# First feed-forward layer by seven block products in place of eight, summed in PSUM

## The chip, the cores and the metric

The kernel runs on one core of a Trainium2 chip. The metric is the device time of one execution in microseconds (us), the median of three runs. Engines are named as the profile names them: PE (TensorE matmuls), PEld (its weight loads), DVE (VectorE), ACT (ScalarE), POOL (GpSimd), SP (SyncE, which issues DMAs). L123 is line 123 of the kernel.

## The reference

A linear attention gives `x` (2304 tokens of 512), a layer of eight experts picks one expert per token, and a feed-forward pair with a gelu in the middle gives the output:

```python
x = _moe_ref(x=attention(q, k, v, omega), w_gate, w1, w2)   # one of 8 experts per token, 512 -> 1024 -> 512
h = x @ w_in                                                # 2304 x 512 by 512 x 2048
g = h * (1.0 / (1.0 + np.exp(-1.702 * h)))
return (g @ w_out).astype(np.float32)                       # 2304 x 2048 by 2048 x 512
```

`w_in` and `w_out` come as 64-bit floats.

## The kernel before

The program has three stages: attention, the experts, and the two feed-forward layers. Each product of float32 quality is three matmuls: an operand is split into a rounded high half (ACT copies it as type fp32r) and the low half that is left (DVE subtracts, `split`, L825 and L826), and high × high, high × low and low × high are summed in PSUM (`mm3`, L123).

The experts (`moe_gen`) go through four batches of 576 tokens in halves of 288. At the end of a half `y` is multiplied by the gate (DVE, L756), ACT rounds it to `yh` (L759), POOL, in the last batch DVE, makes `yl` (L761), and SP stores both in `y_dram` (L766).

The first layer (`first`) takes one of 16 feature tiles of 128 (`wi`) and one of five chunks of tokens (512, 512, 512, 480, 288 columns) and runs 4 × 3 matmuls into one bank of sums, `f_ps`. ACT applies the gelu into `g` (L1016) and stores `g` in `g_dram` (L1017) from its own DMA queue. 80 such pieces make 960 matmuls. Seven banks of PSUM take turns as `f_ps`, and four buffers as `g`. The first few pieces are allowed to run while the experts are still at work, and the scheduler puts them there.

The second layer (`second`, L1070) already uses seven products for eight on 2 × 2 blocks: operands `gs` are sums and differences of blocks of `g` (tile `gt`, loaded by SP from `g_dram`), split by ACT and DVE, and the weights `wo` are seven mixes of the blocks of `w_out`.

Two sorts of jobs prepare this beside the matmuls. `prep_in` loads two tiles of `w_in` (`raw`), decodes the 64-bit floats on DVE (L804, L808, L811, into `dec`) and splits them into `wi`. `prep_out` loads two tiles of `w_out`, decodes them into `z`, mixes the blocks on POOL and stores seven results in `wo_dram`. `prep_w` reads these back and splits them. `load_y` loads a chunk of `y`. A `Runner` moves such jobs on: the program calls it between pieces of the layer, and a job says after how many calls it wants to go on (`yield 6`). All this sets the program order; a scheduler then orders each engine's instructions by priorities and dependences, `behind` keeps an instruction after the last n of its engine, and buffers with the same tag wait for one another (a tile whose tag is in use waits until its last reader is done).

## Time and profile before

| | |
|---|---|
| median of 3 runs | 788.44 us (787.87 to 788.46) |
| profiled execution | 786.61 us, of which the span of the trace is 784.8 us |
| granted clock of the PE, mean over the span | 0.991 of full speed |
| busy share of the span | PE 97%, PEld 91%, DVE 58%, ACT 39%, POOL 23% |
| start of the last expert matmul, last first-layer matmul | 402, 597 us |

The profiled execution is one of its own, so its durations are set against its own time. A granted clock of 1.00 in a stretch is the 2.4 GHz level. Busy shares are means over the three stages. The matmuls' shown durations overlap (the PE is pipelined), so the price of a row of equal matmuls is read from the spacing of their starts.

### The profile page before, as it was taken

What the parts mean: (1) busy time and instruction counts of PE and PEld (TensorE: products, weight loads), DVE (VectorE), ACT (ScalarE), POOL (GpSimd) and SP (SyncE); (2) the same over time, 40 slices, a digit from 0 to 9 for tenths busy, and PEclk for the clock granted to TensorE, in tenths of its full rate; (3) what the DMA queues carried; (4) which work ended last, traced back from release to release, by engine and by line L of the source; (5) the groups of instructions that cost most, each with busy time, mean ns of one, the idle gap of its engine ahead of it and who ended that gap; (6) DMA issues with size and microseconds to landing.
All of it is one profiled execution on the core that took longest, in us unless ns stands there. A gap on an engine that the chain in (4) does not pass through costs nothing.

```text
span 784.8 us, 14258 instructions
## 1 busy us (share of the span) xinstructions
PE 761.8 (97%) x5538; PEld 711.5 (91%) x5538; DVE 453.6 (58%) x1026; ACT 306.4 (39%) x575; POOL 178.8 (23%) x134
## 2 busy tenths in 40 slices
PE   7998899999999999999999999999999999999996
PEld 6877799999999999999998888888889999999996
DVE  5867876586775262644623756530135877777761
ACT  5545563454423342442212322532344433333340
POOL 3564296539402450110002433000000000000000
PEclk9999899999999999999999999999999999999998
DMA  5447676258723430458879999942575444444411
GB/s 160 120 120 179 183 214 161 81 152 234 138 73 104 144 105 31 147 160 291 288 261 346 329 381 342 357 157 101 173 222 175 135 134 136 135 134 134 134 28 30
DMA packets 150185, 136.00 MB, mean 173 GB/s; under 512 B 60768, under 2 KB 131680, under 8 KB 149216
## 3 DMA queue, kind: packets, MB, share of 16 engines
q1 hardware_dynamic: 138592, 116.16, 49.2%
q10 hardware_dynamic: 11520, 18.88, 6.6%
q8 instruction: 45, 0.74, 0.4%
q14 instruction: 28, 0.23, 0.1%
HBM read 83.41 MB, written 45.11 MB: 164 GB/s over the span
## 4 chain that ended last, share of the span: by engine, by line
PE 80%; DMA 7%; DVE 5%; issue 4%; POOL 1%; ACT 1%; SPq 1%; POOLq 0%; DVEq 0%; ACTq 0%
PE f_ps L123 24%; PE m_ps L123 18%; PE qa L1070 12%; PE qm L1070 6%; PE w_ps L123 3%; PE pb L1070 3%; PE kv_ps L385 3%; PE num L427 2%; DMA st<-in_moe_w_dram 2%; DMA gt<-g_dram 1%; PE pr L327 1%; DMA m<-in_q_dram 1%; PE tq L413 1%; DMA m<-in_k_dram 1%; PE pr L333 1%
## 5 line engine op out<-in xcount | busy, mean ns | idle before, releaser
L123 PE MATMUL f_ps<-y,wi 128*128 128x512 f32 (+2 forms) x960 | 199.2, 369 | 0.0
L123 PEld LDWEIGHTS f_ps<-y,wi 128*128 128x128 f32 x960 | 169.8, 188 | 28.3
L1070 PE MATMUL qa<-wo,gs 128*128 128x256 f32 x864 | 107.3, 282 | 0.0
L1070 PEld LDWEIGHTS qa<-wo,gs 128*128 128x128 f32 x864 | 104.9, 190 | 0.1
L1016 ACT ACTIVATE g<-f_ps 128x512 f32<-128x512 f32 (+2 forms) x80 | 44.0, 552 | 102.8 <-PE f_ps L123 83.6
L123 PE MATMUL m_ps<-xh,wh 128*128 128x288 f32 x256 | 78.9, 308 | 2.7 <-DVE h1l L706 1.7
L123 PE MATMUL m_ps<-xh,wl 128*128 128x288 f32 x256 | 76.8, 300 | 0.0
L123 PE MATMUL m_ps<-xl,wh 128*128 128x288 f32 x256 | 76.5, 299 | 0.0
L658 POOL TENSOR_TENSOR wl<-st,wh 128x1024 fp32r<-128x1024 f32 x23 | 54.5, 2376 | 44.7 <-ACT wh L656 44.7
L825 ACT ACTIVATE gs<-s 128x1024 fp32r<-128x1024 f32 x27 | 28.6, 1060 | 75.9 <-DVE s L1055 63.1
L342 DVE TENSOR_REDUCE small<-pr 128x4 f32<-128x512 f32 (+1 forms) x80 | 51.1, 639 | 10.8 <-PE pr L334 6.5
L706 DVE SCALAR_TENSOR_TENSOR h1l<-m_ps,h1h 128x288 fp32r<-128x288 f32 x64 | 28.8, 454 | 48.4 <-ACT h1h L703 48.2
L1070 PE MATMUL qm<-wo,gs 128*128 128x256 f32 x432 | 54.5, 283 | 0.4 <-DVE u L1086 0.4
L1070 PEld LDWEIGHTS qm<-wo,gs 128*128 128x128 f32 x432 | 52.8, 190 | 0.6 <-DVE u L1086 0.6
L123 PEld LDWEIGHTS m_ps<-xh,wh 128*128 128x128 f32 x256 | 48.7, 190 | 3.9 <-DVE h1l L706 2.3
L656 ACT ACTIVATE wh<-st 128x1024 fp32r<-128x1024 f32 (+1 forms) x33 | 34.0, 1031 | 41.7 <-DMA st<-in_moe_w_dram 23.3
L123 PEld LDWEIGHTS m_ps<-xl,wh 128*128 128x128 f32 x256 | 48.8, 190 | 0.2
L123 PEld LDWEIGHTS m_ps<-xh,wl 128*128 128x128 f32 x256 | 48.7, 190 | 0.0
L123 PE MATMUL m_ps<-h1h,wh 128*128 128x288 f32 x160 | 48.6, 305 | 0.0
L826 DVE TENSOR_TENSOR gs<-gt,gs 128x1024 fp32r<-128x1024 f32 x36 | 44.0, 1222 | 7.5 <-ACT gs L825 7.0
L123 PE MATMUL m_ps<-h1h,wl 128*128 128x288 f32 x160 | 47.8, 300 | 0.0
L123 PE MATMUL m_ps<-h1l,wh 128*128 128x288 f32 x160 | 47.7, 299 | 0.0
(156 smaller groups left out, 1422.7 us busy)
## 6 DMA issues: line engine op xcount, KB each, us to landing
gt<-g_dram SPq DMA_DIRECT2D x16, 1024.0 KB, 7.4
st<-in_moe_w_dram SPq DMA_DIRECT2D x31, 512.0 KB, 4.3
g_dram<-g ACTq DMA_DIRECT2D x48, 256.0 KB, 5.1
raw<-in_moe_w_in_dram SPq DMA_DIRECT2D x16, 512.0 KB, 5.8
raw<-in_moe_w_out_dram SPq DMA_DIRECT2D x16, 512.0 KB, 6.1
wo<-wo_dram SPq DMA_DIRECT2D x7, 1024.0 KB, 8.3
y<-y_dram SPq DMA_DIRECT2D x6, 1024.0 KB, 10.7
wo_dram<-z SPq DMA_DIRECT2D x8, 768.0 KB, 5.5
```

Of the source, the lines that this page charges most:

```text
L123: ins = nc.tensor.matmul(out=ps, lhsT=a, rhs=b, start=start and n == 0, stop=stop and n == 2)
L327: nc.tensor.matmul(out=ps[:, :, h2], lhsT=xT[:, (2 * pr + h2) * 2 + t0 // 2], rhs=wbd)
L342: nc.vector.tensor_reduce(out=pm, in_=ps[:, :w], axis=AX.X, op=ALU.max, negate=on_act)
L385: nc.tensor.matmul(out=kv_ps[:, h, :], lhsT=kp[j // 2][:, j % 2, h2, :], rhs=vm[:, h, t, :], start=(t == 0), stop=False,)
L427: nc.tensor.matmul(out=ps[:n, c, h2, :], lhsT=lhsT, rhs=kv[:, h, :])
L656: nc.scalar.activation(out=hi[:, :, s], in_=st[:, :, s], func=ACTF.Copy)
L658: eng.tensor_tensor(out=lo[:, :, s], in0=st[:, :, s], in1=f32(hi)[:, :, s], op=ALU.subtract)
L706: nc.vector.scalar_tensor_tensor(out=hl[:, f], in0=ps, scalar=0.0, in1=f32(hh[:, f]), op0=ALU.max, op1=ALU.subtract)
L825: nc.scalar.activation(out=hi, in_=src, func=ACTF.Copy)
L826: nc.vector.tensor_tensor(out=lo, in0=src, in1=f32(hi), op=ALU.subtract)
L1016: nc.scalar.activation(out=g, in_=ps, func=ACTF.Gelu_apprx_sigmoid)
L1070: ins = nc.tensor.matmul(out=ps, lhsT=x[:, f], rhs=w[i][:, f], start=start and f + m == 0, stop=f == NP - 1 and m == 2, skip_group_check=True,
```

## The change

Now the first layer too takes seven products for eight. The 2 × 2 blocks are: two feature tiles (j and j + 8, 128 features each), two halves of the 512 inputs, and two halves of 384 of a set of 768 tokens. A group (j, t) of the new `first` computes both feature tiles for set t: seven products (`PAIRS`) of 2 × 3 matmuls of 384 columns, 24 groups in all, 1008 matmuls. The sums of products are made in PSUM: product 1 in bank `qa` is copied by ACT into a second bank (`qn` or `qu`), products 6, 5 and 3 go on summing in `qa`, product 7 is copied out as `qs`, and DVE adds `qs` to `qa` once into bank `qt` (where product 4 goes on) and once into a tile `g`. The gelus go to two `g` tiles of 768 columns, `glo` and `ghi`, of a ring of three buffers, each stored whole. Two groups run interleaved. Three marking matmuls ahead of them let the sums go on in banks that an engine has written.

The weights are mixed and split by `prep_ins` (seven blocks per group of tiles, mixes on DVE for j of 0 and 1, else on POOL). `y` is now stored once in float32, without `yh` and `yl`; `prep_y` loads a set, mixes it into seven blocks on DVE and splits each, set 0 while the experts are at work, set 1 in memory that becomes free when they end. `prep_outs` replaces `prep_out` with a fixed pace, and the operands of the second layer take over the memory of sets and weights as they become free (`after_group`), two of the weight sets and three operand buffers only behind the last group. In the diff, lines of plain renaming are left out.

```diff
+    NH = 3 * P
+    NSET = NT // (2 * NH)
+    OUT_PACE = 6
...
-                def rest(y=y, yh=yh, yl=yl, dt=dt, hf=hf):
-                    nc.scalar.activation(out=yh, in_=y, func=ACTF.Copy)
-                    eng = nc.vector if b == B - 1 else nc.gpsimd
-                    eng.tensor_tensor(out=yl, in0=y, in1=f32(yh), op=ALU.subtract)
-                def store(yh=yh, yl=yl, dt=dt, hf=hf):
-                    for x, n, ch, o in pieces(b * S + hf * HS, HS):
-                        for i, t in enumerate((yh, yl)):
-                            nc.sync.dma_start(
-                                out=y_dram[ch][i][dt * P:(dt + 1) * P, o:o + n], in_=f32(t[:, x:x + n])
-                            )
-                lag(LAG_M, rest)
-                lag(3, store)
+                def store(y=y, dt=dt, hf=hf):
+                    x = 0
+                    while x < HS:
+                        ch, o = divmod(b * S + hf * HS + x, NH)
+                        n = min(HS - x, NH - o)
+                        nc.sync.dma_start(out=y_dram[ch][dt * P:(dt + 1) * P, o:o + n], in_=y[:, x:x + n])
+                        x += n
+                lag(2, store)
...
+    PAIRS = {
+        1: (W11, Y11), 2: (W12, Y21), 3: (WS4, Y22), 4: (W22, YT4), 5: (WS1, YT1), 6: (WS2, YT2), 7: (WS3, YT3),
+    }
...
+    def prep_ins():
+        for j in range(NP):
+            after = 4 if j < 2 else 0
+            raws = [load_raw(slots["ly"], 0, f, after) for f in (j, j + NP)]
+            yield IN_PACE
+            dec = slots["dec"].tile([P, 4, HALF], F32, tag="dec", name="dec", bufs=1)
+            mix = raws[0].bitcast(F32).rearrange("p (o c) -> p o c", c=HALF)
+            for n in range(2):
+                decode(dec[:, 2 * n:2 * n + 2].rearrange("p o c -> p (o c)").bitcast(I32), raws[n], HOLD)
+                yield 1
+            s1, s2, s4 = (mix[:, i] for i in range(3))
+            eng = nc.gpsimd if j > 1 else nc.vector
+            tt(eng, s1, dec[:, WS3], dec[:, W22], ALU.add)
+            tt(eng, dec[:, WS3], dec[:, W11], dec[:, WS3], ALU.subtract)
+            tt(eng, s2, s1, dec[:, W11], ALU.subtract)
+            tt(eng, s4, dec[:, W12], s2, ALU.subtract)
+            yield 3 if j > 1 else 1
+            while j % 3 >= len(slots["wi"]) or (j > 2 and through[j - 3] < NSET):
+                yield 1
+            pool, tag = slots["wi"][j % 3]
+            t = pool.tile([P, 14 * HALF], F32R, tag=tag, name="wi", bufs=1)
+            w = t.rearrange("p (s o c) -> p s o c", s=2, o=7)
+            for o, x in ((slice(0, 2), dec[:, 0:2]), (slice(2, 4), dec[:, 2:4]), (slice(4, 7), mix[:, 0:3])):
+                split(w[:, 0, o], w[:, 1, o], x)
+                yield 1
+            wi_t[j] = (w[:, 0], w[:, 1])
...
+    def prep_outs():
+        raws = slots["raw_o"]
+        def load(j):
+            for n, f in enumerate((j, j + NP)):
+                nc.sync.dma_start(out=raws[n], in_=w_out[f * P:(f + 1) * P, :])
+        load(0)
+        for j in range(NP):
+            yield OUT_PACE
+            z = slots["z"][:, j % 2]
+            zi = z.bitcast(I32)
+            for n in range(2):
+                decode(zi[:, 2 * n:2 * n + 2].rearrange("p a c -> p (a c)"), raws[n], HOLD)
+                yield 1
+            if j + 1 < NP:
+                load(j + 1)
+            for o, a, b, op in O_MIX:
+                tt(nc.gpsimd, z[:, o], z[:, a], z[:, b], op)
+            yield 2
+            nc.sync.dma_start(out=wo_dram[0, :, j], in_=z[:, 0])
+            nc.sync.dma_start(out=wo_dram[1:7, :, j].rearrange("o p d -> p o d"), in_=z[:, 2:8])
+            outs[0] += 1
...
+        x = slots["ly"].tile([P, 7, 2, NH], F32, tag="yt", name="yt", bufs=1)
+        for o, k, c in ((Y11, 0, 0), (YT3, 0, 1), (Y22, 1, 1), (Y21, 1, 0)):
+            ins = nc.sync.dma_start(
+                out=x[:, o], in_=y_dram[2 * t + c][k * DM // 2:(k + 1) * DM // 2].rearrange("(k p) n -> p k n", p=P)
+            )
+            behind(ins, after)
+        yield (6, 6, 13)[t]
+        eng = nc.vector
+        behind(tt(eng, x[:, YT1], x[:, YT3], x[:, Y11], ALU.subtract), HOLD)
+        tt(eng, x[:, YT3], x[:, Y22], x[:, YT3], ALU.subtract)
+        yield 1
+        tt(eng, x[:, YT2], x[:, Y22], x[:, YT1], ALU.subtract)
+        tt(eng, x[:, YT4], x[:, Y21], x[:, YT2], ALU.subtract)
+        while not home:
             yield 1
...
+        y = home[0]
+        for o in (YT3, YT2, Y11, Y21, YT1, YT4, Y22):
             yield 1
+            split(y[:, 0, o], y[:, 1, o], x[:, o], HOLD)
+        y_t[t] = (y[:, 0], y[:, 1])
...
+        home1.append(set_tile(hp, 1))
+        slots["wi"].append((hp, "wi2"))
+        jobs.queue.append(prep_y(2, [set_tile(hp, 2)]))
...
+        def marked(tag):
+            ps = bank_of(tag, 1, NH)
+            nc.tensor.matmul(out=ps, lhsT=y_t[0][0][:, 0, 0, 0:P], rhs=y_t[0][0][:, 0, 0])
...
+            def gelu(o, x):
+                nc.scalar.activation(out=o, in_=x, func=ACTF.Gelu_apprx_sigmoid)
+            c0, c1 = slice(0, NH), slice(NH, 2 * NH)
+            pa = bank_of("a", 3, NH)
+            product(1, pa, True)
+            pb = bank_of(("n", "u")[turns[0] % 2], 1, NH)
+            turns[0] += 1
+            nc.scalar.activation(out=pb, in_=pa, func=ACTF.Copy)
+            yield
+            pq = bank_of("m", 2, NH)
+            product(7, pq, True)
+            qs = hp.tile([P, NH], F32, tag="qs", name="qs", bufs=2)
+            nc.scalar.activation(out=qs, in_=pq, func=ACTF.Copy)
+            yield
+            product(6, pa, False)
+            pf = bank_of("t", 1, NH)
+            tt(nc.vector, pf, pa, qs, ALU.add)
+            yield
+            product(2, pb, False)
+            glo = hp.tile([P, 2 * NH], F32, tag="ob", name="g", bufs=3)
+            gelu(glo[:, c0], pb)
+            yield
+            product(5, pa, False)
+            ghi = hp.tile([P, 2 * NH], F32, tag="ob", name="g", bufs=3)
+            tt(nc.vector, ghi[:, c1], pa, qs, ALU.add)
+            yield
+            product(4, pf, False)
+            gelu(ghi[:, c0], pf)
+            gelu(ghi[:, c1], ghi[:, c1])
+            nc.scalar.dma_start(out=g_dram[t][1][j], in_=ghi)
+            yield
+            product(3, pa, False)
+            gelu(glo[:, c1], pa)
+            nc.scalar.dma_start(out=g_dram[t][0][j], in_=glo)
+            through[j] += 1
...
+        order = [(0, 0), (1, 0), (0, 1), (1, 1), (2, 0), (2, 1), (0, 2), (1, 2), (2, 2)]
+        order += [(j, t) for j in (3, 4) for t in range(NSET)]
+        order += [(j, t) for t in range(NSET) for j in (5, 6, 7)]
...
+            g = first(j, t)
+            for mine in (1, 0, 1, 0, 0, 1, 1):
+                if mine:
+                    next(g)
+                elif live is not None:
+                    next(live[0], None)
+                jobs()
+            if live is not None:
+                after_group(*live[1])
+            live = (g, (j, t))
+        for _ in range(3):
+            next(live[0], None)
             jobs()
+        wp.release()
+        wq = tc.alloc_tile_pool(name="wq", bufs=1)
+        gs_homes += [wq.tile([P, GSW], F32R, name=f"gs{i}") for i in range(2)]
+        g_homes.append(wq.tile([P, 2, NP, 2 * P], F32, name="gt1"))
+        p = hp.tile([P, SETW], F32R, tag="y2", name="p2", bufs=1)
+        jobs.queue += [prep_w(5, p[:, 0:WO], 3, 0), prep_w(6, p[:, WO:2 * WO], 4, 0)]
+        gs_homes.append(p[:, 2 * WO:2 * WO + GSW])
+        gts = {1: load_g(1)}
```

What this does to the order on the engines is shown at three places. **PE inside the first layer**, before: one feature tile (`f_ps`) with four chunks of tokens, named by their `y` tile, and the first matmul of the next.

```order
L123 MATMUL f_ps<-y_4658,wi 128x512 [waits Activation_49]
L123 MATMUL f_ps<-y_4658,wi 128x512 x11
L123 MATMUL f_ps<-y_4788,wi 128x512 [waits Activation_49]
L123 MATMUL f_ps<-y_4788,wi 128x512 x11
L123 MATMUL f_ps<-y_5071,wi 128x480 [waits Activation_49]
L123 MATMUL f_ps<-y_5071,wi 128x480 x11
L123 MATMUL f_ps<-y_5266,wi 128x288 [waits Activation_49]
L123 MATMUL f_ps<-y_5266,wi 128x288 x11
L123 MATMUL f_ps<-y_4656,wi 128x512 [waits Activation_49]
```

And after, six products of two interleaved groups, one on set 2 (`y_5142`), the next on set 0 (`y_3929`); `qa`, `qm`, `qt` and `qn` are banks. In turn these are product 5 of the first group, 7 of the second, 4 and 3 of the first, 6 and 2 of the second.

```order
L1068 MATMUL qa<-y_5142,wi 128x384 [waits DVE_49]
L1068 MATMUL qa<-y_5142,wi 128x384 x5
L1068 MATMUL qm<-y_3929,wi 128x384 x6
L1068 MATMUL qt<-y_5142,wi 128x384 [waits Activation_49]
L1068 MATMUL qt<-y_5142,wi 128x384 x5
L1068 MATMUL qa<-y_5142,wi 128x384 [waits DVE_49]
L1068 MATMUL qa<-y_5142,wi 128x384 x5
L1068 MATMUL qa<-y_3929,wi 128x384 [waits Activation_49]
L1068 MATMUL qa<-y_3929,wi 128x384 x5
L1068 MATMUL qn<-y_3929,wi 128x384 x6
```

Before, a piece waited only at its start, for the gelu that emptied its bank; after, products 5 and 3 wait for the DVE add that reads their bank, 6 for ACT's copy out of it, and 4 for an ACT instruction too.

**ACT at the end of the experts**, before: the last halves of `h1`, the last `yh`, then the first gelus of pieces whose matmuls are partly done.

```order
L703 ACTIVATE h1h<-m_ps 128x288 [waits PE_49] x4
L759 ACTIVATE yh<-y 128x288 [waits DMAHW0_49,DVE_49,Activation_49]
L759 ACTIVATE yh<-y 128x288 [waits DMAHW2_49,DVE_49,Activation_49]
L759 ACTIVATE yh<-y 128x288 [waits DMAHW0_49,DVE_49,Activation_49]
L759 ACTIVATE yh<-y 128x288 [waits DMAHW2_49,DVE_49,Activation_49]
L1016 ACTIVATE g<-f_ps 128x512 [waits DMAHW4_49,DMAHW5_49,DMAHW3_49,DMAHW6_49,DMAHW1_49,DMAHW7_49,DVE_49,PE_49]
L1016 ACTIVATE g<-f_ps 128x512
L1017 DMA g_dram<-g 128x512 [waits Activation_49] x2
```

And after (`y_5141` is set 1, `yt` its mixed blocks, `wi` from `dec` or `raw` the third tile of weights).

```order
L694 ACTIVATE h1h<-m_ps 128x288 [waits PE_49] x4
L1083 ACTIVATE qn<-qa 128x384 [waits PE_49]
L810 ACTIVATE wi<-dec 128x512 [waits DMAHW3_49,DMAHW4_49,DMAHW2_49,DMAHW5_49,DMAHW1_49,DMAHW6_49,DMAHW0_49,DMAHW7_49,DVE_49,Activation_49]
L810 ACTIVATE y_5141<-yt 128x768
L1088 ACTIVATE qs<-qm 128x384 [waits PE_49]
L810 ACTIVATE wi<-dec 128x512 [waits Pool_49]
L810 ACTIVATE y_5141<-yt 128x768
L810 ACTIVATE wi<-raw 128x768 [waits DMAHW0_49,Pool_49]
L810 ACTIVATE y_5141<-yt 128x768
L810 ACTIVATE y_5141<-yt 128x768 [waits DMAHW7_49]
```

Between the last `h1h` and the copies `qn` and `qs`, which the PE's products wait for, there now stand splits into memory that the last stores and readers of the experts hold.

**DVE among the decodes of `w_out`**, before: only decodes (`z`, `dec`), in the first layer nothing of the layer itself.

```order
L804 TENSOR_SCALAR z<-raw 128x512 [waits DMAHW2_49]
L811 SCALAR_TENSOR_TENSOR dec<-raw,dec 128x512 [waits DVE_49]
L808 SCALAR_TENSOR_TENSOR z<-raw,z 128x512 [waits DVE_49]
L811 SCALAR_TENSOR_TENSOR z<-raw,z 128x512 [waits DVE_49]
L804 TENSOR_SCALAR z<-raw 128x512 [waits DMAHW1_49,DMAHW4_49,DMAHW0_49,Pool_49]
L808 SCALAR_TENSOR_TENSOR z<-raw,z 128x512 [waits DVE_49]
L811 SCALAR_TENSOR_TENSOR z<-raw,z 128x512 [waits DVE_49]
L826 TENSOR_TENSOR wi<-dec,wi 128x512 [waits Activation_49] x2
```

And after (`pz` is the new place of `z`, `raw_o` the loaded weights).

```order
L788 TENSOR_SCALAR pz<-pz 128x512 [waits DMAHW5_49,DVE_49]
L793 SCALAR_TENSOR_TENSOR pz<-pz 128x512 [waits DVE_49]
L796 SCALAR_TENSOR_TENSOR pz<-pz 128x512 [waits DVE_49]
L788 TENSOR_SCALAR pz<-raw_o 128x512 [waits DMAHW7_49]
L793 SCALAR_TENSOR_TENSOR pz<-raw_o,pz 128x512 [waits DVE_49]
L857 TENSOR_TENSOR g<-qa,qs 128x384 [waits DMAHW7_49,PE_49]
L796 SCALAR_TENSOR_TENSOR pz<-raw_o,pz 128x512 [waits DVE_49]
L857 TENSOR_TENSOR qt<-qa,qs 128x384 [waits PE_49,Activation_49]
L857 TENSOR_TENSOR g<-qa,qs 128x384 [waits DMAHW4_49,PE_49]
L788 TENSOR_SCALAR pz<-pz 128x512 [waits DMAHW1_49]
```

The adds `qt` and `g` of the first layer now stand in DVE's order between decodes that wait for loads, and each add into `g` waits for a DMA, the store that last read its buffer.

## Rows read from the trace of the kernel before

**Rows 1.** The page's first line.

```profile
span 784.8 us, 14258 instructions
```

**Rows 2.** Windows: length, busy (x count) PE PEld DVE ACT POOL, PEclk, DMA, GB/s.

```profile
340.00:360.00 20.00, 18.33 (x135) 17.69 (x134) 12.89 (x21) 8.82 (x16) 2.75 (x2) 1.00 0.76 240
...
402.00:597.00 195.00, 195.00 (x946) 167.05 (x945) 81.50 (x108) 66.59 (x104) 27.56 (x32) 1.00 0.77 262
...
620.00:778.00 158.00, 158.00 (x1328) 158.00 (x1327) 111.85 (x123) 58.95 (x69) 0.00 (x0) 1.00 0.37 110
440.00:460.00 20.00, 20.00 (x98) 17.14 (x97) 16.61 (x28) 5.59 (x10) 7.35 (x8) 1.00 0.99 341
```

**Rows 3.** PE's groups by shape, 402 to 597.1: busy us, mean ns, idle.

```profile
L123 PE MATMUL f_ps<-y,wi 128*128 128x512 f32 x563 | 129.9, 390 | 0.0
L123 PE MATMUL f_ps<-y,wi 128*128 128x480 f32 x192 | 43.4, 379 | 0.0
L123 PE MATMUL f_ps<-y,wi 128*128 128x288 f32 x192 | 27.4, 295 | 0.0
```

**Rows 4.** Timeline of PE: start, length; the first and the thirteenth.

```profile
386.63 0.29 PE L123 MATMUL m_ps<-xh,wh 128*128 128x288 f32 x1
...
388.22 0.29 PE L123 MATMUL w_ps<-h1h,wh 128*128 128x288 f32 x1
```

**Rows 5.** Chain of waits through 320 to 404: start, length, what.

```profile
323.69 6.51 DMA y_dram<-yl
...
346.84 1.53 POOL yl L761
...
348.95 4.23 DMA st<-in_moe_w_dram
...
353.21 1.07 ACT wh L656
...
355.90 0.04 issue
```

**Rows 6.** PE's groups by shape, 372 to 402.

```profile
L123 PE MATMUL f_ps<-y,wi 128*128 128x512 f32 x13 | 3.6, 393 | 0.0
```

**Rows 7.** ACT's and DVE's groups over the span: busy, mean ns, idle before.

```profile
L825 ACT ACTIVATE gs<-gt 128x1024 fp32r<-128x1024 f32 x36 | 37.9, 1052 | 18.3 <-PE qa L1070 11.9 <-DVE gt L1055 3.5 <-DMA gt<-g_dram 1.7
L703 ACT ACTIVATE h1h<-m_ps 128x288 fp32r<-128x288 f32 x64 | 25.7, 403 | 41.0 <-PE m_ps L123 39.4 <-PE w_ps L123 1.3
L825 ACT ACTIVATE wi<-dec 128x512 fp32r<-128x512 f32 x16 | 9.4, 627 | 10.1 <-PE f_ps L123 5.1 <-DVE dec L811 4.5 <-ACT g L1016 0.5
...
L826 DVE TENSOR_TENSOR gs<-gt,gs 128x1024 fp32r<-128x1024 f32 x36 | 44.0, 1222 | 7.5 <-ACT gs L825 7.0
L826 DVE TENSOR_TENSOR wi<-dec,wi 128x512 fp32r<-128x512 f32 x16 | 12.0, 789 | 31.2 <-ACT wi L825 31.2
L756 DVE TENSOR_TENSOR y<-m_ps,gb 128x288 f32<-128x288 f32 x20 | 9.0, 452 | 15.8 <-PE m_ps L123 13.7 <-POOL yl L761 2.0
```

**Rows 8.** Timelines: SP's last `y` store, ACT's first gelu.

```profile
405.83 0.32 SPq L766 DMA_DIRECT2D y_dram<-yl  x1
...
409.06 0.60 ACT L1016 ACTIVATE g<-f_ps 128x512 f32<-128x512 f32 x1 [3.74 <-PE f_ps L123]
```

**Rows 9.** `g` stores, median us to landing: 440:480 (two), 520:560, 565:575.

```profile
g_dram<-g ACTq DMA_DIRECT2D x11, 256.0 KB, 5.1
...
g_dram<-g ACTq DMA_DIRECT2D x3, 144.0 KB, 5.5
...
g_dram<-g ACTq DMA_DIRECT2D x10, 256.0 KB, 2.0
...
g_dram<-g ACTq DMA_DIRECT2D x3, 256.0 KB, 6.5
```

**Rows 10.** Waits of DVE, 402 to 600: us in total, times, longest.

```profile
DVE z L804 <- DMA raw<-in_moe_w_out_dram: 20.1, 10, 5.0
```

**Rows 11.** The page's DMA issues: count, KB, median us to landing.

```profile
raw<-in_moe_w_out_dram SPq DMA_DIRECT2D x16, 512.0 KB, 6.1
```

More of the change, by code (lines that the diff above doesn't have):

```diff
@@ L807, in decode @@
         )
+        behind(ins, n)
         nc.vector.scalar_tensor_tensor(
@@ L894, in load_y @@
[L894 to L902 removed]
+    slots = {}
+    W11, W12, WS3, W22, WS1, WS2, WS4 = range(7)
+    Y11, Y21, Y22, YT3, YT1, YT2, YT4 = range(7)
```

274 lines of the change are left out of this document (123 added, 151 removed).

## The prediction

> **What bounds the kernel now.** Read the windows by stage first [rows 2]: from 402 to 597 us the PE is busy for 195.00 of 195.00 us, and from 620 to 778 us for 158.00 of 158.00, at a granted clock of 1.00 (the 2.4 GHz level). The whole of the two feed-forward layers is therefore PE time, and only less PE work, or a new wait, moves the end. Next come the shapes in the first of these stretches [rows 3]: 563 matmuls of 512 columns, 192 of 480 and 192 of 288; with 13 earlier ones [rows 6] that makes the layer's 960. Their mean durations overlap, so the price is taken from spacing: twelve matmuls of 288 columns start 1.59 us apart from first to thirteenth [rows 4], 0.133 us each. The 192 narrow ones thus take 25.5 us, which leaves 169.5 us for 755 with 503.9 columns on average, 0.2245 us each. On the line through these two points 384 columns cost 0.174 us.
>
> **The products, −22.3 us.** Before, the layer takes 195.0 us and 13 × 0.228 = 3.0 us ahead of it, together 198.0. After: 8 weight tiles × 3 token groups × 7 products × 6 matmuls = 1008 of 384 columns, 175.2 us, and the three marking matmuls 0.5. The difference is −22.3. A price of 0.160 us (384 columns at 2.4 GHz, nothing on top) would give −36, which no row supports, as all three widths lie on one line; the term is good to about 1 us.
>
> **y in float32, −1.2 us.** It removes `yh` on ACT and `yl` on POOL and half of the y stores. One gap of the PE hangs on them: 20.00 − 18.33 = 1.67 us between 340 and 360 us [rows 2]. The chain of that stretch goes back from the late weights (ACT `wh`, the load of `st`) over the POOL's `yl` to a y store [rows 5]. In the new program the SP queue reaches that load without a POOL step ahead of it. I take 1.2 of the 1.67; the bounds are 0 and 1.7.
>
> **The tail of the experts without filler, +1.2 us.** Thirteen first-layer matmuls now run between 372 and 402 us [rows 6] and fill about 2.9 us. After, none can stand there. Between the two halves of the last batch VectorE has four `y` products, two small mixes, a wide `wi` split and four low halves of set 0 and one of `wi` ahead of the first `h1l`; by 0.46, 0.4, about 1.0 and 0.8 us each ([rows 7], widths between the rows interpolated) that is 8.0 us. The PE needs that `h1l` after 52 matmuls of 0.133, so 6.9. I take 1.2; bounds 0 and 2.9.
>
> **Opening the layer, +3.8 us.** Set 1, the third weight tile and `qs` lie on memory of the experts. ACT's first split into it waits for the last y store and stands ahead of `qs` in ACT's order. Today the same hand-over takes from 405.83 (last store) to 409.06 us (first `g`), 3.2 us [rows 8], hidden since seven banks of sums can wait. After: last store 0.7 us behind the last expert matmul, ACT free at 3.9, weight split 0.63, set-1 split 0.84 (between 0.627 and 1.052 [rows 7]), `qs` 0.5: 5.9. VectorE's `qt` add stands behind a low half that ends at 6.4, and ends at 7.0. Product 5 of group 1 was due at 5 × 1.04 = 5.2: stall 1.8. Product 6 of group 2 then falls due at 11.2, but its ACT copy stands behind six splits and a gelu and ends at 12.6: 1.4. Its `qt` add stands behind five low halves: 0.6. Bounds 1 and 7: the interval in which copies find ACT free, and a store that lands like the slow ones of [rows 9].
>
> **The ring of three output buffers, +6.0 us.** This is the term that decides. A group takes 7 × 1.04 = 7.3 us and fills two tiles of 768 columns out of three. The add into `ghi` takes the buffer of the `glo` stored one group before, and product 3 waits for that add, since it goes on summing in the bank that the add reads. From product 3 of one group to product 3 of the next the PE has six other products, 6.26 us. In these must fit: gelu 0.48, add 0.56 (both between rows of 288 and 512 columns [rows 7]), hand-overs of 0.02 to 0.05 us [rows 5] and the 0.16 us by which a matmul's end trails the next one's start [rows 4], 1.4 together, and the landing of `glo`. So a landing up to 4.9 us costs nothing, and each us above costs a us per group. A store of 256 KB lands in 2.0 us where the DMA is nearly empty, 5.1 where it is full, and one of 144 KB there in 5.5 [rows 9]: the crowd sets it, not the size. Will it be crowded? Reading and writing back `w_out` is 1.97 MB per ten calls of the job runner (10.4 us, 189 GB/s), `g` 0.79 MB per group (108), `w_in` 1.05 MB per three groups (48): 345 GB/s from the sixth to the seventeenth group, against 341 GB/s at a share of 0.99 today [rows 2]. So I take 5.5 us for ten of these twelve groups: 10 × 0.6 = 6.0. Bounds: 0 at 2.0 us; 12 × 1.6 = 19 at the 6.5 us of [rows 9].
>
> The Trainium skill, "DMA: Bandwidth & Descriptors", on the anatomy of one DMA, gives about 2.0 us plus the bytes at 436 GB/s. For 384 KB that is an estimate of 2.9 us, and the ring would be free. The empty stretch (2.0 us for 256 KB) is near that rule, the full one is not, so the row decides here.
>
> **Crossing to the second layer, +2.5 us.** Two weight sets, three operand buffers and the next `g` load get their memory only when the last group is done. On VectorE seven operations of 1.22 us [rows 7], one of them behind 2 MB of loads, stand up to the low half that product 6 of block 0 needs: 2.2 + 8.5 = 10.7 us after the end, against three products of 24 matmuls, 8.6 us (158 us for 1328 [rows 2]). That is 2.1, and 0.4 for the last two weight sets. Bounds 0 and 6.
>
> **The sum.** −22.3 − 1.2 + 1.2 + 3.8 + 6.0 + 2.5 = −10.0 us. The profiled execution took 786.6 us with a span of 784.8 [rows 1], so its counterpart should show a span near 774.8. The median of the runs lies 1.8 us above the profiled time; −10.0 on 788.44 gives 778.4 us.
>
> **The rivals.**
> - *The ring is free*, because the paced `w_out` work leaves gaps into which the stores fall: landings below 4.9 us. For it: 2.0 us from 520 to 560 us [rows 9]; against it, the 345 GB/s above. Time: 788.4 − 16.0 = 772.4 us, and 767 if opening and crossing also come at their lower ends. The page's 2.9 us would bring this case about.
> - *VectorE stands still for `w_out`.* Today its decodes wait 20.1 us in ten waits, the longest 5.0, for these loads [rows 10], and nobody minds. After, the adds of the first layer stand between these decodes on the same queue. An add has two products, 2.09 us, less its own 0.56 and 0.25 of hand-over, so 1.25 us of slack. Ten waits of 2.0 exceed it by 7.5 us in all: 786 us. Against it: each load is issued some eight runner calls, 8.3 us, ahead of its decode, and takes 6.1 us [rows 11].
> - *Slower.* The ring again, at a higher price: two stores of 384 KB leave within 1 us on one queue, and the second waits for the first as well. All other terms sum to −16.0, so over twelve groups it decides from 4.9 + 16.0/12 = 6.2 us of landing on. At 6.5 us, as from 565 to 575 us [rows 9], the ring costs 19 us: 791.6 us. Against it: a stretched group asks for less bandwidth, which shortens the landing again.
>
> **How the numbers follow.** Forecast 0.51 (its own range 773 to 784), ring free 0.24, VectorE held 0.12, slower 0.13. The range from 767 to 788 leaves out the upper part of the slow case and little else. 0.2% of 788.4 is 1.6 us, which is about what this kernel's runs can tell from nothing. Below 786.8: all of the first two cases and two thirds of the third, 0.82. Within 1.6 us: 0.07. Above 790.0: 0.11.
>
> **What the changed profile would show.** The first layer's matmuls spaced 0.174 us apart inside a product (wrong if 0.19). PE idle of 3 to 5 us in its first 16 us, ended by a VectorE add or an ACT copy. Then, in the groups among the `w_out` decodes, a gap of about 0.6 us ahead of product 3, ended by the add into `g`, which itself waited for a `g_dram` store of 5 to 6 us; no such gap in groups without those loads. At the end of the layer a wait for a low half of `gs`. The prediction fails if the stores land in 3 us (too slow a forecast) or if every group shows a gap of 1.5 us (too fast a one).

## The result

The changed kernel takes 795.5 us (median of 6 runs, 792.33 to 797.46), the kernel before 788.2 us on the same chip: a ratio of 1.0089, interval 1.0061 to 1.0116. It is slower, where 778.4 us and a gain were forecast, and outside the range. The profiled execution took 792.33 us with a span of 790.5, among the fastest of its six; its span is 5.7 us longer than that of [rows 1], and that difference is taken apart here (the medians lie 7.3 us apart).

Stages are measured alike in all kernels: the first layer from 0.13 us (one spacing) behind the start of the last expert matmul to the first matmul of the second layer, the second from there to the end of its last matmul. Before, they take 195.4 and 181.1 us; after, 191.3 and 191.6. The change wins 4.1 us where it was made (7.0 with the 13 matmuls that ran ahead of the layer before) and loses 10.5 behind it.

The windows of the changed kernel, columns as in [rows 2]; the first four are the first layer, the last two lie in the second:

```profile
401.00:428.00 27.00, 24.12 (x135) 22.88 (x133) 19.64 (x28) 16.39 (x30) 5.17 (x8) 1.00 0.63 211
428.00:490.00 62.00, 61.62 (x349) 61.14 (x350) 40.22 (x62) 30.71 (x61) 16.61 (x19) 1.00 0.75 243
490.00:540.00 50.00, 45.74 (x246) 43.82 (x245) 41.39 (x61) 21.96 (x44) 27.41 (x30) 0.97 0.83 283
540.00:592.00 52.00, 50.09 (x283) 49.13 (x282) 18.98 (x24) 26.45 (x48) 0.34 (x1) 1.00 0.73 263
602.00:607.00 5.00, 0.00 (x0) 0.00 (x0) 2.25 (x2) 0.20 (x1) 0.00 (x0) 0.87 1.05 425
607.00:612.00 5.00, 4.83 (x22) 4.84 (x23) 4.65 (x5) 0.00 (x0) 0.00 (x0) 0.50 0.78 270
```

PE, busy throughout before [rows 2], now has gaps in three of the four parts of the first layer, and from 602 to 607 us it does nothing at all. The timeline of PE names what ended each gap (start, length, and in brackets the idle time ahead and its releaser):

```profile
408.64 1.32 PE L1068 MATMUL qa<-y,wi 128*128 128x384 f32 x6 [2.11 <-DVE qt L857]
428.23 2.38 PE L1068 MATMUL qa<-y,wi 128*128 128x384 f32 x12 [0.86 <-DVE g L857]
509.74 2.00 PE L1068 MATMUL qa<-y,wi 128*128 128x384 f32 x6 [1.81 <-DVE qt L857]
531.79 2.39 PE L1068 MATMUL qa<-y,wi 128*128 128x384 f32 x12 [1.91 <-DVE g L857]
569.89 2.36 PE L1068 MATMUL qa<-y,wi 128*128 128x384 f32 x12 [0.79 <-DVE g L857]
586.00 2.37 PE L1068 MATMUL qa<-y,wi 128*128 128x384 f32 x12 [1.09 <-DVE g L857]
607.17 5.06 PE L1169 MATMUL qa<-p,gs 128*128 128x256 f32 x22 [5.76 <-DVE gs L811]
615.94 1.69 PE L1169 MATMUL qm<-p,p 128*128 128x256 f32 x12 [0.56 <-DVE p L811]
618.87 1.57 PE L1169 MATMUL qm<-p,p 128*128 128x256 f32 x11 [1.24 <-DVE p L811]
```

Every gap is ended by VectorE. In the quiet middle, from 428.23 us on, 222 matmuls start within 39.1 us, 0.1761 us each, so 1008 of them are worth 177.5 us; the other 13.8 us of the layer are waits and what the clock loses after them. This difference, the time since the layer's start less 0.1761 us per matmul, is called the lag below.

Most of these adds are late because VectorE did other work first. ScalarE's first split into the memory of the experts, then four places of VectorE, in the changed kernel (start, length, in brackets idle time and what ended it):

```profile
405.75 0.63 ACT L810 ACTIVATE wi<-dec 128x512 fp32r<-128x512 f32 x1 [2.88 <-DMA y_dram<-y]
```

```profile
506.52 0.43 DVE L788 TENSOR_SCALAR dec<-raw 128x512 int32<-128x512 int32 x1 [2.03 <-DMA raw<-in_moe_w_in_dram]
...
530.58 0.69 DVE L811 TENSOR_TENSOR wi<-dec,wi 128x512 fp32r<-128x512 f32 x1 [2.38 <-ACT wi L810]
531.19 0.55 DVE L857 TENSOR_TENSOR g<-qa,qs 128x384 f32<-128x384 f32 x1
...
560.84 0.56 DVE L857 TENSOR_TENSOR g<-qa,qs 128x384 f32<-128x384 f32 x1 [4.03 <-DMA g_dram<-g]
...
585.39 0.56 DVE L857 TENSOR_TENSOR g<-qa,qs 128x384 f32<-128x384 f32 x1 [5.09 <-DMA g_dram<-g]
```

Of the adds that PE had to wait for, only the last two waited themselves for a store of `g`; the add at 531.19 stood behind a low half of weights that waited for its split. The store that ended the last wait, as ScalarE issues it and in the chain of waits:

```profile
578.10 0.33 ACTq L1105 DMA_DIRECT2D g_dram<-g  x1
...
578.10 7.20 DMA g_dram<-g
```

L1105 is the store of `ghi`, L1109 that of `glo`.

The largest gap, at the crossing, in the chain of waits (start, length, what):

```profile
593.09 11.57 DMA gt<-g_dram
...
604.75 0.13 DVE s L1155
...
605.89 1.23 DVE gs L811
...
607.17 4.86 PE qa L1169 x21
```

Block 1's first sum (`s`, L1155) stands in VectorE's order ahead of the low half `gs` that product 6 of block 0 needs, and waits for block 1's `gt`, which takes 11.6 us to land. SP asks for 2 MB of `gt`, 2 MB of weights and the first MB for block 2 between 592.7 and 599 us. The two weight sets, asked for behind `gt`, take 14.1 us (median of the two, 1 MB each):

```profile
p<-wo_dram SPq DMA_DIRECT2D x2, 1024.0 KB, 14.1
```

### The profile page after: what moved, and what is told of

Its sections match the earlier page's. It is cut to its first block, busy times and chain, and to the rows that moved or that the text cites. A ratio compares the mean times of both kernels' runs of the same rounds, so it can differ in the third digit from the quotient of the medians.

```text
span 790.5 us, 14448 instructions
## 1 busy us (share of the span) xinstructions
PE 747.5 (95%) x5589; PEld 720.4 (91%) x5589; DVE 517.3 (65%) x1122; ACT 340.0 (43%) x643; POOL 181.4 (23%) x134
## 4 chain that ended last, share of the span: by engine, by line
PE 36%; DVE 8%; DMA 7%; issue 3%; ACT 2%; POOL 1%; ACTq 0%; DVEq 0%; SPq 0%; POOLq 0%
PE qa L1169 12%; PE qm L1169 6%; PE qa L1068 5%; PE m_ps L125 4%; PE pb L1169 3%; PE w_ps L125 2%; DMA g_dram<-g 2%; DMA gt<-g_dram 1%; PE qt L1068 1%; PE qm L1068 1%; DMA pg<-g_dram 1%; PE qu L1068 1%; DVE wi L811 1%; DVE p L811 1%; DMA y_dram<-y 1%
## 5 line engine op out<-in xcount | busy, mean ns | idle before, releaser
L1068 PE MATMUL qa<-y,wi 128*128 128x384 f32 x576 | 112.4, 341 | 9.4 <-DVE g L857 5.0
L1068 PEld LDWEIGHTS qa<-y,wi 128*128 128x128 f32 x576 | 101.0, 189 | 14.0 <-DVE g L857 7.1
L125 PE MATMUL m_ps<-xh,wl 128*128 128x288 f32 x256 | 76.1, 297 | 0.0
L1169 PE MATMUL qa<-p,gs 128*128 128x256 f32 x360 | 47.4, 291 | 5.8 <-DVE gs L811 5.8
L1169 PEld LDWEIGHTS qa<-p,gs 128*128 128x128 f32 x360 | 45.9, 198 | 6.0 <-DVE gs L811 6.0
L1169 PE MATMUL qa<-p,p 128*128 128x256 f32 x360 | 45.3, 282 | 0.3 <-DVE p L811 0.3
L1169 PEld LDWEIGHTS qa<-p,p 128*128 128x128 f32 x360 | 43.9, 190 | 0.5 <-DVE p L811 0.5
L694 ACT ACTIVATE h1h<-m_ps 128x288 fp32r<-128x288 f32 x64 | 25.7, 404 | 43.1 <-PE m_ps L125 43.0
L857 POOL TENSOR_TENSOR pz<-pz 128x256 f32<-128x256 f32 x32 | 29.7, 949 | 63.0 <-DVE pz L796 63.0
L429 PE MATMUL num<-kv,qpT 128*128 128x65 f32 (+1 forms) x320 | 39.0, 265 | 2.3 <-ACT qpT L417 1.4
```

The lines of the kernel that those rows point to most:

```text
L125: ins = nc.tensor.matmul(out=ps, lhsT=a, rhs=b, start=start and n == 0, stop=stop and n == 2)
L429: nc.tensor.matmul(out=ps[:n, c, h2, :], lhsT=lhsT, rhs=kv[:, h, :])
L694: nc.scalar.activation(out=hh[:, f], in_=ps, func=ACTF.Relu)
L857: return eng.tensor_tensor(out=out, in0=a, in1=b, op=op)
L1068: ins = nc.tensor.matmul(out=ps, lhsT=w[:, a, ks], rhs=y[:, b, kk], start=start and kk + m == 0, stop=kk == 1 and m == 2, skip_group_check ...
L1169: ins = nc.tensor.matmul(out=ps, lhsT=x[:, f], rhs=w[i][:, f], start=start and f + m == 0, stop=f == NP - 1 and m == 2, skip_group_check=True,
```

## The experiments

The stages are from one profile each, so a few tenths of a us between two rows tell nothing; the ratio is to the kernel before on the same chip, and two kernels whose intervals overlap are hardly told apart by it; what a step did is then read from the gaps in the traces.

| kernel | median us (before) | ratio, interval | first, second layer us |
|---|---|---|---|
| changed kernel | 795.5 (788.2) | 1.0089 [1.0061, 1.0116] | 191.3, 191.6 |
| e1_pin | 789.1 (785.3) | 1.0041 [1.0009, 1.0072] | 192.3, 187.4 |
| e2_pin_loads | 789.3 (785.3) | 1.0062 [1.0032, 1.0091] | 191.6, 191.0 |
| e3_ring4 | 787.3 (785.3) | 1.0034 [1.0008, 1.0060] | 185.3, 193.3 |
| e4_no_w_out_work | 805.9 (785.3) | 1.0253 [1.0191, 1.0314] | 209.4, 192.4 |
| e5_loads_late_pin | 790.9 (786.7) | 1.0052 [1.0024, 1.0080] | 190.2, 186.8 |
| e6_all_three | 786.6 (786.7) | 0.9989 [0.9963, 1.0015] | 188.2, 187.6 |
| e8_mixes_on_gpsimd | 784.2 (786.7) | 0.9974 [0.9952, 0.9996] | 185.7, 188.4 |
| e9_out_pace_8 | 797.9 (786.7) | 1.0143 [1.0126, 1.0159] | 198.5, 191.5 |
| e10_crossing_in_order | 784.7 (787.4) | 0.9969 [0.9939, 0.9999] | 185.3, 187.2 |
| e11_in_pace_8 | 784.2 (787.4) | 0.9974 [0.9950, 0.9998] | 190.4, 185.4 |
| e12_weights_on_gpsimd | 788.0 (787.4) | 1.0001 [0.9976, 1.0025] | 185.5, 188.3 |
| e13_first_copy_first | 785.9 (787.4) | 0.9989 [0.9966, 1.0011] | 185.2, 189.9 |
| e14_block0_first | 780.7 (786.6) | 0.9932 [0.9906, 0.9957] | 185.8, 185.8 |

**e1_pin.** An instruction is kept behind another of its engine, without a wait (`after_ins` below stands for this):

```diff
+                if k == 1 and len(kept_lows) <= 8:        # block 1's first two sums
+                    after_ins(ins, kept_lows[3])           # the low half for product 6 of block 0
```

> Only the crossing to the second layer is changed: block 1's first sum on VectorE stands behind the low half that product 6 of block 0 needs, so that it no longer waits for block 1's load of g. Theory order (that one place in VectorE's queue is the whole of the loss at the crossing): the 5.8 us gap ahead of product 6 goes, and with it the fall of the clock; about 8 us faster than the changed kernel, 787 to 788 us. Theory crowd (6 MB are asked for within 6 us at the end of the first layer, so the last two weight sets land late whatever VectorE's order): the gap moves on to products 2 and 4, and 3 to 5 us are won, 790 to 792 us.

The second layer falls by 4.2 us. The gap ahead of product 6 shrinks from 5.8 to 0.6 us, but 0.7 us come up in product 2 and 2.3 + 0.7 ahead of and in product 4: the crowd's forecast by its size (3.8 us by ratios). Here ScalarE waited 1.9 us for the load of the last weights (at 608.6 us), so in this order of the loads bytes did arrive late.

**e2_pin_loads.** As e1, with a call of the job runner ahead of `gts = {1: load_g(1)}`, so that the two weight sets are asked for first.

> As e1_pin, and the loads of the last two weight sets stand ahead of block 1's load of g on SP's queue. Theory order: no more than e1_pin, about 8 us under the changed kernel. Theory crowd: clearly better than e1_pin, no gap above 1 us left between 597 and 625 us, 8 to 10 us under the changed kernel, 785 to 787 us.

Neither came: 191.0 us, with 5.3 us of idle PE ahead of product 4, ended by the VectorE add that empties its bank. Ahead of that add VectorE stood 3.1 us for a low half of block 1, whose split on ScalarE waited for the now later load, and 0.6 us for block 1's sum. So with the weights loaded first, places in the engines' order hold block 0.

**e3_ring4.**

```diff
-            glo = hp.tile([P, 2 * NH], F32, tag="ob", name="g", bufs=3)
+            glo = hp.tile([P, 2 * NH], F32, tag="ob", name="g", bufs=4)
```

and likewise `ghi` and `ob`; two constants of 0.5 KB per partition move to the memory of the attention to make room.

> The ring of output buffers has four tiles instead of three (two constants moved out of the way for the space); nothing else. Theory ring (the stores of g set the waits of the first layer, as forecast at 6 us): the waits of the add into g go from the groups among the w_out work, 5 to 6 us faster than the changed kernel, 789 to 790 us. Theory queue (VectorE's own order: decodes, and splits that wait for loads, ACT or GpSimd, stand ahead of the adds): only the wait at 585 us goes, 1 to 2 us, 793.5 to 794.5 us.

The first layer takes 185.3 instead of 191.3 us. VectorE's waits in that layer, of the changed kernel:

```profile
DVE qt L857 <- PE qa L1068: 31.7, 13, 3.7
DVE g L857 <- DMA g_dram<-g: 12.5, 4, 5.1
DVE wi L811 <- ACT wi L810: 11.8, 6, 4.6
```

and with four buffers:

```profile
DVE qt L857 <- PE qa L1068: 33.2, 12, 3.7
DVE g L857 <- PE qa L1068: 16.1, 8, 2.5
DVE wi L811 <- ACT wi L810: 11.9, 6, 4.9
```

The waits for `g_dram` stores are gone, the others stay. The time is what theory ring foretold: four profiles with three buffers (the changed kernel, e1, e2, e5) have first layers of 190.2 to 192.3 us, seven with four buffers and the same paces (e3, e6, e8, e10, e12 to e14) 185.2 to 188.2, some 5 us apart. But the lag shows where they differ: 1.1 us at 428 us, 1.4 near 531, 0.3 at 561, 0.95 at 570 and 1.25 at 586 (times of the changed kernel). Only the two steps of 0.3 and 1.25 go with adds that wait for a store (the two other such waits, 3.2 us at 439 and 0.2 at 503, held nothing). The others go with another order on VectorE: at 428 the add stands behind four sums of `yt`, at 570 behind block 0's sums, and the add at 531 behind a waiting low half of weights, while e3 has it ahead:

```profile
523.70 0.55 DVE L857 TENSOR_TENSOR g<-qa,qs 128x384 f32<-128x384 f32 x1
526.16 0.69 DVE L811 TENSOR_TENSOR wi<-dec,wi 128x512 fp32r<-128x512 f32 x1 [1.92 <-ACT wi L810]
```

So most of the gain goes, as far as the traces show, with the order that the scheduler chooses when there is one buffer more, not with shorter waits for stores. What remains in e3 above 177.5 is 7.8 us: 3.1 at the opening, and nearly all of the rest from 485 to 535 us, in waits for adds that stand in VectorE's queue.

**e4_no_w_out_work.**

```diff
+        nc.gpsimd.memset(slots["z"], 0.25)
...
-                decode(zi[:, 2 * n:2 * n + 2].rearrange("p a c -> p (a c)"), raws[n], HOLD)
...
-                tt(nc.gpsimd, z[:, o], z[:, a], z[:, b], op)
```

> Leaves out the decoding of w_out on VectorE and its mixes on GpSimd: loads and stores of w_out stay as they are, but what is stored is a constant, so the output is not the reference's. Theory ring: the traffic is the same, so the waits for the stores of g stay and the time falls by less than 2 us. Theory queue: VectorE has nothing between the adds but the w_in work, the gaps between 485 and 532 us go with the fall of the clock there, 5 to 8 us faster than the changed kernel, 788 to 790 us.

It went the other way, for both theories, 13 us slower than the changed kernel by ratios (1.0253 against 1.0089, times 788). With no decode and no mix between a load of `w_out` and the stores, these follow each other faster, and they crowd (370 GB/s below; the changed kernel has 315 from 450 to 470 us). Its window:

```profile
450.00:470.00 20.00, 9.24 (x43) 8.92 (x43) 1.68 (x3) 4.62 (x11) 0.00 (x0) 0.84 1.06 370
```

and VectorE's waits in the layer:

```profile
DVE g L857 <- DMA g_dram<-g: 32.7, 6, 11.7
```

PE does 9.2 us of work in 20, VectorE 1.7: no engine is busy, the adds wait for stores up to 11.7 us. So the traffic can make the ring the bound; this run shows that for a heavier traffic than the changed kernel's, and does not part the two theories for that kernel. A side result, VectorE's decodes by their mean (from 440 to 540 us), first in the changed kernel, then here, without GpSimd's mixes beside them:

```profile
L793 DVE SCALAR_TENSOR_TENSOR dec<-raw,dec 128x512 int32<-128x512 int32 x8 | 6.8, 849 | 0.1
```

```profile
L793 DVE SCALAR_TENSOR_TENSOR dec<-raw,dec 128x512 int32<-128x512 int32 x8 | 5.5, 693 | 0.3
```

**e5_loads_late_pin.** As e2, but block 1's first sum stands behind the two adds that follow product 6 (`after_ins(ins, puts[1])`).

> The last two weight sets are loaded ahead of block 1's g, and block 1's first sum on VectorE stands behind the two adds with which block 0 empties its banks after product 6 (in e2 that sum, waiting for the now later load, held back exactly these adds). Theory order and crowd together: with the loads in the order of need and no waiting sum ahead of block 0's adds, the second layer takes 182 to 184 us from its first matmul to its last (191.6 in the changed kernel, 187.4 in e1, 191.0 in e2), some 8 us less than the changed kernel, ratio to before 0.998 to 1.001. If DMA bandwidth alone is the limit there, the gap moves to block 1's first products and the layer stays at 187 or more.

186.8 us for the second layer, where 182 to 184 were expected. Now ScalarE shows the same fault:

```profile
610.33 1.06 ACT L810 ACTIVATE gs<-gt 128x1024 fp32r<-128x1024 f32 x1 [6.78 <-DMA gt<-g_dram]
611.30 1.04 ACT L810 ACTIVATE p<-s 128x1024 fp32r<-128x1024 f32 x1
612.24 0.36 ACT L1186 ACTIVATE pg<-qa 128x256 f32<-128x256 f32 x1
```

The split of block 1's first operand waits 6.8 us for its load, and block 0's copy after product 6 (`pg<-qa`) stands behind it.

**e6_all_three** joins e3 and e5.

> e5_loads_late_pin and the ring of four buffers of e3_ring4. If the two losses (ring 6 us, crossing 8 us) are separate, they add up: first layer 185 to 186 us, second 182 to 184, 14 us less than the changed kernel, ratio to before 0.990 to 0.993, faster than the kernel before. If the stores of g that the ring releases crowd the loads at the crossing, part is given back: ratio 0.995 or more.

The gains add up in the second layer (187.6) and mostly in the first (188.2; a wait at 510 us is 2.5 us, where e3 has 0.3). The ratio is 0.9989, no change that can be told.

**e8_mixes_on_gpsimd.**

```diff
-            eng = nc.gpsimd if j > 1 else nc.vector
+            eng = nc.gpsimd
```

> e6_all_three, and the mixes of the first two weight tiles, made while the experts end, go from VectorE to GpSimd. If VectorE's work for the coming layer is what delays the low halves of the experts, the 1.6 us gap at some 377 us shrinks to under 0.5 us, and the time falls by about 1 us against e6_all_three; if GpSimd's slower mixes come too late for the first groups, the opening of the first layer grows instead.

The gap shrinks from 1.64 us in e6 to 1.17, less than expected; the opening's first gap falls from 2.1 to 1.5. The difference of the medians (2.4 us) is more than these two explain, and the intervals of e6 and e8 overlap.

**e9_out_pace_8** sets `OUT_PACE = 8` in the changed kernel, with its ring of three.

> The changed kernel with its w_out work spread over a third more calls (pace 8 in place of 6), ring of three. Theory ring and crowd: less traffic per us in the middle of the first layer, so the waits there shrink by 2 to 3 us; but w_out work then lasts into the last groups, next to the loads of weights and g, and can cost as much there. Net within 2 us of the changed kernel, ratio to before 1.006 to 1.011. If ratio 1.003 or less, the pace was the cause, not the size of the ring.

Slower than expected: 198.5 us for the first layer. The PE waits 3.8 us at 492 and 5.0 at 575 us for adds into `g`. No store held these: the first add stood behind a decode that waited 4.6 us for its load of `w_in`, the second behind operations for the second layer that waited for a split (1.6 us) and the load of `g` (1.5). It is VectorE's queue, with loads that come late for it, that decides here, and not the ring.

**e10_crossing_in_order.** As e8, and

```diff
+                if k == 1 and not firsts:
+                    after_ins(hi, u2s[0])        # ScalarE: behind block 0's copy after product 6
...
+                if k == 2:
+                    after_ins(ins, stores[0])    # SP: behind block 0's first store
```

> e8_mixes_on_gpsimd, and at the crossing nothing of block 1 stands ahead of block 0 any more: on ScalarE the split of block 1's first operand comes behind block 0's copy after product 6 (in e6 it waited 6.9 us for its load and held that copy and the splits of the last weights), and SP issues block 2's load of g behind block 0's first store, so that block 1's g does not share the DMA engines with it (it took 15 us to land in e6). Theory (in-order queues holding block 0 for block 1's late load is the whole of the loss at the crossing): second layer 181.5 to 183 us (188.4 in e8), ratio to before 0.989 to 0.992. Rival (the bytes themselves: 2 MB of weights after the last group cannot be there in time): the gap ahead of products 4 and 3 stays, layer at 185 or more, ratio 0.994 or more.

187.2 us. VectorE's row at that place:

```profile
602.19 0.42 DVE L1201 TENSOR_TENSOR ob<-qa,pg 128x256 f32<-128x256 f32 x1
604.33 1.23 DVE L1167 TENSOR_TENSOR s<-gt 128x1024 f32<-128x1024 f32 x1 [1.72 <-DMA gt<-g_dram]
605.48 2.35 DVE L812 TENSOR_TENSOR p<-p 128x1024 fp32r<-128x1024 f32 x2
```

Once more the sum of block 1 waits for its load, now ahead of a low half of weights that product 4 needs. By layer time alone the rival (bytes) would have been read out of this; e14 tells them apart. With the weights asked for ahead of `gt`, as in e2 and in all runs from e5 on but e9, they land in half the time of the changed kernel (this row is of e10):

```profile
p<-wo_dram SPq DMA_DIRECT2D x2, 1024.0 KB, 7.2
```

**e11_in_pace_8** sets `IN_PACE = 8` in e10.

> e10_crossing_in_order with two more runner calls between the load of two tiles of w_in and their decoding (8 in place of 6). If the remaining waits of product 5 at some 507 us come from a decode on VectorE that stands ahead of the add and waits for its load of w_in (2.0 us in the changed kernel), that gap of 1.6 to 2.5 us goes: first layer 1.5 to 3 us shorter than in e10. If VectorE's own work is too dense there (decodes take 1.1 instead of 0.7 us beside GpSimd's mixes), the wait only moves and the layer stays within 1 us.

The wait moves and grows: 190.4 us, 5.1 us more than e10, where neither theory had a longer layer. There are 2.6 us at 532 us for a split of the weights that now comes too late, and waits at 427 and 436 us that e10 does not have. That the time is still that of e10 comes from the second layer (185.4) and above all from the experts: the gap at 377 us is gone in e11, and from the end of the attention's last count to the last expert matmul it takes 72.1 us, 4.5 us less than in e10. In e10 VectorE makes four low halves for the coming layer between the last product `y` of a half and the next `h1l`; in e11 they stand behind that `h1l`.

**e12_weights_on_gpsimd.**

```diff
-                split(w[:, 0, fs], w[:, 1, fs], f32(w[:, 1, fs]), HOLD)
+                split(w[:, 0, fs], w[:, 1, fs], f32(w[:, 1, fs]), HOLD, nc.gpsimd if i in (4, 6) else nc.vector)
```

> e10_crossing_in_order, and the low halves of weight sets four and six of the second layer are made by GpSimd, which stands idle there, instead of VectorE. Theory (with nothing waiting in front, the rest of the loss at the crossing, 6 us in e10, is VectorE's own row of operations of 1.2 us each between the end of the first layer and product 4): the waits ahead of products 6 and 4 of block 0 (1.2 and 2.3 us in e10) shrink to under 1 us together, second layer 183 to 185 us (187.2), ratio to before 0.992 to 0.995. Rival (the landing of the last two weight sets): the waits stay within 0.5 us of those in e10.

The wait ahead of product 6 grows to 2.9 us. VectorE, and below it GpSimd, in e12:

```profile
592.85 1.22 DVE L812 TENSOR_TENSOR p<-pg,p 128x1024 fp32r<-128x1024 f32 x1
593.99 3.42 DVE L1167 TENSOR_TENSOR s<-s,pg 128x1024 f32<-128x1024 f32 x1
597.34 3.40 DVE L812 TENSOR_TENSOR p<-pg,p 128x1024 fp32r<-128x1024 f32 x1
600.66 1.21 DVE L812 TENSOR_TENSOR gs<-s,gs 128x1024 fp32r<-128x1024 f32 x1
...
593.64 6.01 POOL L812 TENSOR_TENSOR pw<-pw 128x1024 fp32r<-128x1024 f32 x2 [52.41 <-ACT pw L810]
```

Two VectorE operations moved away ahead of product 6 cost two others 2.2 us each: while GpSimd works, one of 1.22 us takes 3.4.

**e13_first_copy_first.** The memory for set 1 and the third weight tile is handed to the jobs one product later, so that ScalarE's first `qs` stands ahead of their splits.

> e12_weights_on_gpsimd, and at the opening of the first layer ScalarE's first splits into the experts' memory come behind the first copy qs instead of ahead of it; qs itself lies in that memory and still waits for the last store of y. By the forecast's opening term (store landed 3.9 us after the end of the experts, then 0.63 and 0.84 us of splits ahead of qs): the first gap of the layer, 1.6 us in e10, falls by about 1.4 us, and the time by 1 to 2 us against e12. If the gap does not move, what is waited for there is VectorE (low halves ahead of the add), not the copy.

The lag behind 0.1761 us per matmul, after the layer's first 60 matmuls, falls from 2.05 us in e12 to 0.55: the opening term is read rightly. But 1.2 us come back at 417 us, where an add stands behind six low halves of set 1; the first layer is only 0.3 us shorter (185.2 against 185.5). Against e12 the median is 2.0 us lower, but the intervals overlap.

**e14_block0_first** is e10 and e13 without GpSimd's low halves. The jobs are now called until the last weights are made before block 1's first operations are, so that these can stand behind them:

```diff
+                    after_ins(ins, lows[-1])     # block 1's first sum behind the last weights' low halves
...
+                while step == 6 and not k and seven[step] not in wo_t:
+                    jobs()
```

> e10_crossing_in_order with the copy order of e13, and block 1's first sum on VectorE stands behind all low halves of the last two weight sets as well (in e10 it waited 1.7 us for its g ahead of the second half of a set that product 4 needs); GpSimd makes none of them. Theory order: the wait ahead of product 4 (2.3 us) goes, the 1.2 us ahead of product 6 stays (seven operations of VectorE in a row, as the forecast counted them), second layer 183 to 185 us, ratio to before 0.992 to 0.995. Rival bytes (the weights land too late, 7.2 us for 2 MB beside 2 MB of g): a wait of 1.5 us or more stays ahead of products 4 or 3, layer at 186 or more, ratio 0.996 or more.

VectorE in e14, same place:

```profile
602.45 0.42 DVE L1201 TENSOR_TENSOR ob<-qa,pg 128x256 f32<-128x256 f32 x1
602.79 2.35 DVE L812 TENSOR_TENSOR p<-p 128x1024 fp32r<-128x1024 f32 x2
605.05 0.42 DVE L1201 TENSOR_TENSOR ob<-pb,pg 128x256 f32<-128x256 f32 x1
605.39 1.22 DVE L812 TENSOR_TENSOR p<-p 128x1024 fp32r<-128x1024 f32 x1
606.52 1.22 DVE L1166 TENSOR_TENSOR s<-gt 128x1024 f32<-128x1024 f32 x1
```

No wait is left ahead of products 4 and 3: with the weights asked for first, the bytes were not too late. 1.2 us ahead of product 6 stay, and 2.1 us move into block 1, whose operands are now prepared later, with 1.8 us of low clock behind them (granted 0.66 from 614 to 619 us). The second layer takes 185.8 us, 4.7 more than before the change. By its interval the version is faster than both kernels, by 0.7% than the kernel before, ratio 0.9932.

## Why the prediction was wrong

Term by term, in the profiled span (forecast −10.0, measured +5.7 us):

- **Products, −22.3:** 198.3 us before (195.4 and 13 matmuls ahead) against 177.5, −20.8. The price is 0.1761 us instead of 0.174, small hand-overs included. Right mechanism, 1.5 us too much. (That all widths lie on one line was no finding: the line was drawn through two points, one of them the mean of two widths.)
- **y in float32 and the tail, −1.2 + 1.2:** from the end of the attention's last count (a cast on VectorE, 326.6 us before, 326.2 after) to the last expert matmul it took 72.3 us without the 13 fillers, and takes 75.0: +2.7, with 73.4 to 76.1 in e1 to e4 and 79.4 in e5, so one profile is worth little here. The tail's gap is there (1.64 us at 377 us), somewhat larger than forecast, although the operations that the prediction lists for it add up to 7.6 us by its own prices and not to 8.0. The gain of the smaller stores did not come: one of the two gaps of [rows 2]'s first window shrinks to 0.67 us, and others come up nearby. e8 and e11 bear on it: with the first mixes moved to GpSimd the tail's gap shrinks to 1.17 us, and with the decodes of `w_in` two calls later it goes, and the stretch takes 72.1 us.
- **Opening, +3.8:** the lag is 3.9 us after 132 matmuls, but 1.1 us of it (the wait at 427 us) belong to the ring and are absent with four buffers, so 2.8 is the size. The mechanism is right: ScalarE's first split waited for the last `y` store, and e13, with `qs` ahead of the splits, takes the first gap away.
- **Ring, +6.0:** a fourth buffer is worth some 5 us, so the size came out, but by luck: the mechanism of the sum, an add that waits for a store and holds product 3, costs 0.3 + 1.25 us, in two groups. Two things were wrong in it. The place: in the groups among `w_out` work the stores land in 4.6 to 5.2 us (medians) and hold nothing, and the long waits (4.0 and 5.1 us) come at 561 and 585 us, beside the loads of weights and `g` for the second layer. And the slack: both adds started when the store of `ghi` of the group before had landed (L1105; 6.2 and 7.2 us), not that of `glo`, which leaves a product later; by their costs a landing up to some 5.9 us is free (an estimate from these two), where the sum had 4.9. The other 3.4 us are the order that the scheduler gives VectorE when three buffers are all it has (e3). The Trainium skill, "DMA: Bandwidth & Descriptors", on the anatomy of one DMA, would let a store of 384 KB land in 2.9 us by an estimate; that section is on DMAs issued by GpSimd, while these stores are issued by ScalarE, and their medians of 4.1 to 5.4 us go with the crowded row of [rows 9] instead.
- **VectorE held by its own queue:** it stood among the rivals, with a chance of 0.12, and at nothing in the sum, although its own time (786 us) is the forecast with 7.5 us on top. It does come on top: from 428 to 540 us the lag grows by 7.4 us in the changed kernel, 1.6 us of them PE at the low clock after the wait at 508 us, and by 4.7 us in e3, where no store is waited for. The loads of `w_out`, its premise, were not what was waited for: a decode waited 2.0 us for `w_in`, with the add of 508 us behind it, and a low half 2.4 us for its split. No run takes this loss away: e9 and e11, with other paces, make the layer longer.
- **Crossing, +2.5:** 10.5 us. This is the step that failed. It counted VectorE's seven operations and named the load ahead of one of them, but took that load for landed in time. It takes 11.6 us, beside 3 MB of others. The count itself was good: with no such wait (e14) the low half for product 6 is done 10.1 us after the layer's end, where the sum had 10.7. The changed kernel loses 11.1 us at the crossing and the kernel before 0.6. Of the 11.1, 5.9 are that wait, 2.2 the low clock after it (22 matmuls in 4.86 instead of 2.62 us), and 3.0 the last weights, for which the sum had 0.4. Their splits queue up behind the wait, but they are also late themselves: they land at 607.1 and 609.7 us, and product 4, behind five products of 24 matmuls, was due at some 606.7 (an estimate from the layer's end at 592.4 and 0.119 us per matmul).

Had the last two points been priced as measured (about 5 and 10.5 instead of 0 and 2.5), the sum would have come out 13 us higher, at +3, on the side of the rival that ended slower, though by another mechanism than that rival's. Of the signs that the prediction names, the wait for a low half of `gs` came, nearly three times as long as the 2.1 us priced, and the gaps of 0.6 us among the `w_out` decodes did not. What is left open: which part of the experts' 2.7 us is VectorE's work for the new layer (e11 points to all of it, by one profile).

## What to carry over

When a stage gets shorter, look at the instructions that a scheduler puts at its end for the next stage: any one that waits for a load holds everything behind it on its in-order engine, so price the load's landing among all that is asked for with it, and order the queue by need rather than by readiness (the changed kernel, e2, e5 and e10 each show the same fault one instruction further on). Mechanisms that can all be true belong into the sum, not among rivals that exclude each other. And before a buffer is taken away for space, compare the time between its uses with the landing time in the most crowded stretch, and look at what the scheduler makes of the missing buffer: one more was worth 5 us here, a third of it in waits for stores.
